# Agent attention and a top-1 mixture of experts: narrower margins of two tests, two left tiles less, banks of products issued in one go

## The chip, the core and the metric

The kernel runs on one core of one Trainium2 chip. The metric is the time of the program on the device in microseconds. Before the change it was 717.3 us, the median of three runs (715.77 to 720.54).

## The reference

Four batches of 11456 tokens with 128 channels. An attention through 49 agents is followed by a mixture of eight experts, of which each token takes one.

```python
a2k = softmax(agents @ k.T * scale)        # 49 x 11456
agent_v = a2k @ v                          # 49 x 128
x = softmax(q @ agents.T * scale) @ agent_v
e_idx = argmax(x @ w_gate)                 # one expert a token
out = probs[e_idx] * sigmoid(x @ w_output_gate)[e_idx] * (relu(x @ w1[e_idx]) @ w2[e_idx])
```

All is f32. The expert's hidden layer has 1024 units.

## The kernel before, in words

A token's x is a mean of the 49 rows of agent_v, so all of a batch's tokens lie close to each other. The kernel uses that twice. First, each batch has one expert that nearly all of its tokens choose (`choose`). Second, most hidden units of that expert have the same sign at every token. `units` ranks the 1024 units by how near to a sign change they can come (`k16`, the squared cosine between a unit's weights and the direction of the mean, in steps). The 256 most doubtful units are computed for each token (the main stream: `mm1`, `relu`, `mm2`). All others are folded into one linear product (`linear`).

Whether a token may use this is tested. `q_rest` computes, for each unit of 1024 tokens (8 tiles of 128), eight gate products `lg` into one bank, and then the products `t` with the next 256 units of the rank, two tiles to a bank. `most` (VectorE) and `beyond` (ScalarE) look whether one of these leaves its sign by the margin SLIGHT (lines 345, 377, 378). For the units behind rank 512 a ball bound holds: `limit` makes `lim` from the unit at rank 512, and `route` compares the token's norm with it (line 1357). A token that fails a test, or that chooses another expert, is a *left* token.

Left tokens are gathered by expert into tiles of 128 and computed in f32 with all 1024 units. `left_table` counts them by phase (a phase is a batch here), `left_index` finds a tile's tokens by indirect DMAs on POOL's queue, `left_load` fetches the expert's weights (SP's queue, 2 x 512 KB), `left_front` makes the transpose `let` and the product `lx` (K = 49), `left_back` the eight products `lh`, two ReLUs, eight products `ly` and a scaling, and `left_store` scatters the rows over the output (POOL's queue). PHASES (line 33) says how many tiles of each phase are in the program: 10, 6, 4 and 1. A group that needs more is computed by a loop at the end (lines 2024 to 2035), which is passed over otherwise.

All instructions are emitted by a planner that is written into the kernel. Each piece of work is a generator that yields what its next instruction reads and writes. `can` (line 117) decides by planned times whether it may be issued; PE's side work has slots that `tick` (line 514) gives between the main stream's products. A generator has a priority: left work has LEFT (line 1872), the scoring products 4. So what is issued where, on every engine, follows from these planned times, and a change of one piece moves the pieces behind it. The engines then run their queues in order.

Of the kernel before, what the change touches and what calls it, by code (L numbers as in the profile page):

```python
# [13 lines left out]
ALU = mybir.AluOpType  # L14
# [4 lines left out]
B, N, C, A, E, F = 4, 11456, 128, 49, 8, 1024  # L19
# [4 lines left out]
ACTIVE = NK * P  # L24
CHOSEN = 2 * ACTIVE
# [4 lines left out]
SCALE = 1.0 / float(C) ** 0.5  # L30

LARGE, SMALL, KEEP = 7, 10, 3
PHASES = [(0, 1, 10, 128), (1, 1, 6, 128), (2, 1, 4, 128), (3, 1, 1, 128)]
ORDER = [0, 1, 3, 2]
NG = B * E
BIG = 1048576.0
# [238 lines left out]
def agent_attention_top1_moe(ctx, tc, qT, kT, v, aT, wg, wo, w1, w2, cst, out):  # L275
    nc = tc.nc
    clk = Clock()
    ACT, DVE, POOL = Engine(clk, "ACT", nc.scalar), Engine(clk, "DVE", nc.vector), Engine(clk, "POOL", nc.gpsimd)
    PE, SY = Engine(clk, "PE", nc.tensor), Engine(clk, "SP", nc.sync)
# [32 lines left out]
    def hold(long=False):  # L312

        k = last[0]
        banks[k][0] = False
        if long:
            long_held.append((k, banks[k][1]))
        return k
# [23 lines left out]

    LONG = 3
    SUMMED = (2, 6)
    SLIGHT = 7.0 / 16.0 * 1.02

    kc = cp.tile([P, K_W], F32, name="kc")
    sel = wk.tile([P, A2], F32, name="sel", tag="sel", bufs=1)
# [6 lines left out]
    def load_constants():  # L355
# [20 lines left out]
        POOL.memset(signed[:, 1:2], 0.5)  # L376
        POOL.memset(slight, SLIGHT)
        POOL.memset(passed, -SLIGHT)
        for u in range(3):
# [41 lines left out]
    for i in range(3):  # L421
        t = cp.tile([P, 8, P], F16, name=f"e16_{i}")
# [5 lines left out]
    for i in range(2):  # L428
        t = cp.tile([P, 2, 18], F16, name=f"gs_{i}")
# [3 lines left out]
    for i in range(2):  # L433
        t = cp.tile([P, E, NCOL], F32, name=f"oht_{i}")
# [8 lines left out]

    efd = [dr.tile([n * N, A2], F32, name=f"efd{b0}") for b0, n, _, _ in PHASES]
    cumd = [dr.tile([n * E * P, NCOL], F32, name=f"cumd{b0}") for b0, n, _, _ in PHASES]
    ppid = [dr.tile([n * E, P], F32, name=f"ppid{b0}") for b0, n, _, _ in PHASES]
    avnd = dr.tile([B, A, C], F32, name="avnd")
    ttd = [dr.tile([r, 8], F32, name=f"ttd{b0}") for b0, _, _, r in PHASES]
    ttid = [dr.tile([r, 8], I32, name=f"ttid{b0}") for b0, _, _, r in PHASES]

# [450 lines left out]
    def units(b, ad, w1t, w2t):  # L901
# [3 lines left out]
        t = bank(f"awp{b}")  # L905
        mark = hold()
        tv = t[:, 0:NB * A].rearrange("p (n a) -> p n a", a=A)
# [12 lines left out]
        u = wk.tile([P, NB], F32, name=f"uu{b}", tag="uu")  # L920
# [18 lines left out]
        yield from DVE.q.reciprocal(iq, q)  # L939
        yield from DVE.q.tensor_tensor(u, u, iq, op=ALU.mult)  # L940
        k16 = wk.tile([P, NB], F16, name=f"k16{b}", tag="k16")
        yield from DVE.q.tensor_scalar(k16, u, 1024.0, 1024.0, op0=ALU.mult, op1=ALU.add)
        calm[0] = b == 0
        key = wk.tile([P, NB], F32, name=f"key{b}", tag="key")
        yield from DVE.q.tensor_tensor(key, k16, unit_no, op=ALU.add)
# [11 lines left out]
        for hf in (1, 0):  # L957
# [4 lines left out]
            t, mark = krs[hf]  # L962
            yield "PE", [k16], [t], 1
            for j in range(HB):
                PE.matmul(t[:, j * P:(j + 1) * P], k16[:, hf * HB + j:hf * HB + j + 1].broadcast_to([P, P]), idf16,
                          start=False, stop=(j == HB - 1))
            chain((below_rows, above_rows)[hf](t, mark, rows[hf], (low, pm)[hf], key, nkey, made), b)
        yield from any_bank()
        t = bank(f"cs{b}")
# [32 lines left out]
        for n in range(NB):  # L1002
            yield from DVE.q.tensor_scalar(pm[:, n], places_, rank[:, n:n + 1], sg[:, n:n + 1], op0=ALU.is_equal,
                                           op1=ALU.mult)
# [6 lines left out]
        for j, (x, c) in enumerate(((st["A16"], CHOSEN), (R16, ACTIVE))):  # L1011
            yield from any_bank()
            t = bank(f"wp{b}_{j}")
# [62 lines left out]
    def limit(b, rank, k16):  # L1076

        while not state[b]["w"]:
            yield None
        x = wk.tile([P, NB], F32, name=f"lmx{b}", tag="lmx")  # L1080
        c = wk.tile([P, 1], F32, name=f"lmc{b}", tag="lmc")
        yield from DVE.q.scalar_tensor_tensor(x, rank, float(CHOSEN), k16, op0=ALU.is_equal, op1=ALU.mult, accum_out=c)
        yield from wait_free()
        r = bank(f"lim{b}")
        mark = hold()
        yield from PE.q.matmul(r[:, 0:1], ones, c, start=True, stop=True)
        lim = wk.tile([P, 1], F32, name=f"lim_{b}", tag="lim")

        yield from DVE.q.tensor_scalar(lim, r[:, 0:1], -A / SLIGHT / 1024.0, A / SLIGHT * (2.0 + 0.5 / 1024.0 + 1e-5),
                                       op0=ALU.mult, op1=ALU.add)  # L1090
        release(mark)
        yield from DVE.q.reciprocal(lim, lim)
        state[b]["lim"] = lim
# [96 lines left out]
    def q_rest(b, u, s, mark):  # L1190
        base, pp, nt = UNITS[u]
        me = len(rests)
        rests.append(0)
        r = group_of(b, u)
        off = 8 * (u - r["units"][0])
        e2, lv, tm = (x[0:pp, off:off + nt] for x in (r["e2"], r["lv"], r["tm"]))
        while not home_ready(b, u) or me > 1 and not state.get(0, {}).get("w"):
            yield None
        sv = s[0:pp, 0:nt * A2].rearrange("p (t a) -> p t a", a=A2)[:, :, 0:A]
        while me > 1 and squared[0] < me - 1:  # L1200
            yield None
        m = wk.tile([P, 8], F32, name=f"qm{b}_{u}", tag="qm", bufs=3)
        yield from DVE.q.tensor_reduce(m[0:pp, 0:nt], sv, axis=AX.X, op=ALU.max)
        z = wk.tile([P, 8, A2], F32, name=f"qz{b}_{u}", tag="qz", bufs=2)
        yield from DVE.q.tensor_tensor(z[0:pp, 0:nt, 0:A], sv,
                          m[0:pp, 0:nt].unsqueeze(2).broadcast_to([pp, nt, A]), op=ALU.subtract)
        release(mark)
        if "ef" not in r:
            r["ef"] = wk.tile([P, 24, A2], F32, name=f"ef{b}_{u}", tag=home(b, u), bufs=1)
        ef = r["ef"][:, off:off + 8, :]  # L1210
        ev = ef[0:pp, 0:nt, 0:A]
        yield from ACT.q.activation(ev, z[0:pp, 0:nt, 0:A], AF.Exp, scale=SCALE)
        e16 = e16s[(NU * b + u) % 3]
        yield from ACT.q.copy(e16[0:pp, 0:nt, 0:A], ev)
        yield from LOW.q.tensor_tensor(e16[0:pp, 0:nt, A:2 * A], ev, e16[0:pp, 0:nt, 0:A], op=ALU.subtract)
        yield from POOL.q.tensor_copy(e16[0:pp, 0:nt, 2 * A:P], ev[:, :, AR:A])
        yield from ACT.q.activation(z[0:pp, 0:nt, 0:A], ev, AF.Square)
        while not r["free"]():
            yield None
        yield from DVE.q.tensor_reduce(e2, z[0:pp, 0:nt, 0:A], axis=AX.X, op=ALU.add)  # L1220
        squared[0] += 1
        while me > 0 and rests[me - 1] < 1:
            yield None
        while vacant_turned() is None:
            yield None
        x1 = place(("x1", b, u), vacant_turned()[1], [1024], F16)
        yield from SY.q.dma_start(x1[:, 0:nt * pp].rearrange("p (t c) -> p t c", c=pp), e16[0:pp, 0:nt, :],
                                  transpose=True)
        X1[b, u] = x1
        rests[me] = 1  # L1230
        while not {"gs", "ndom"} <= state.get(b, {}).keys() or (me > 0 and rests[me - 1] < 2):
            yield None
        gs = state[b]["gs"]
        yield from wait_free()
        lg = bank(f"lg{b}_{u}")
        mark = hold()
        for t in range(nt):
            yield from PE.q.matmul(lg[0:pp, t * 36:(t + 1) * 36], x1[:, t * pp:(t + 1) * pp],
                                   gs.rearrange("p k c -> p (k c)"), start=True, stop=True)
        yield from ACT.q.copy(lv.rearrange("p t a -> p (t a)"), lg[0:pp, 0:nt * 36])  # L1240
        release(mark)
        rests[me] = 2
        while not state[b]["w"] or me > 0 and tested[0] < me:
            yield None
        own_ = state[b]["w"][0][0]
        for h in range(0, nt, 2):
            n = min(2, nt - h)
            yield from wait_free()
            t = bank(f"t{b}_{u}_{h}")
            mark = hold()  # L1250
            tv = t.rearrange("p (t k) -> p t k", k=ACTIVE)
            for k in range(n):
                yield from PE.q.matmul(tv[0:pp, k, :], x1[:, (h + k) * pp:(h + k + 1) * pp], own_[:, ACTIVE:CHOSEN],
                                       start=True, stop=True)
            spawn((most, beyond)[h in SUMMED](tm[:, h:h + n], tv[0:pp, 0:n, :], mark, r), 1)
        tested[0] += 1
        r["efs"][u] = ef, me
        if u == r["units"][-1]:
            spawn(route(b, r), 0)
# [38 lines left out]
    def route(b, r):  # L1298
# [8 lines left out]
        e2, tm, lv = r["e2"][:, 0:nt], r["tm"][:, 0:nt], r["lv"][:, 0:nt]  # L1307
# [8 lines left out]
        while not clk.started:  # L1316
# [12 lines left out]
                                 op0=ALU.is_ge, op1=ALU.mult)  # L1329
# [24 lines left out]
            SM[b, u] = smt[:, 8 * (u - u0):8 * (u - u0) + UNITS[u][2]]  # L1354
        dd = tl("dd")
        yield from DVE.q.scalar_tensor_tensor(dd, d256, state[b]["lim"], d256, op0=ALU.mult, op1=ALU.mult)
        yield from DVE.q.scalar_tensor_tensor(dd, e2, SLIGHT, dd, op0=ALU.mult, op1=ALU.is_ge)
        far = rm
        yield from DVE.q.tensor_tensor(far, tm, passed[:, 0:nt], op=ALU.is_gt)
        yield from DVE.q.tensor_tensor(dd, dd, far, op=ALU.max)  # L1360
# [6 lines left out]
        for u in us:  # L1367
            base, pp, k = UNITS[u]
            ef, me = r["efs"][u]
            yield from POOL.q.tensor_copy(ef[0:pp, 0:k, A], T[0:pp, 8 * (u - u0):8 * (u - u0) + k])  # L1370
            r0 = (b - PHASES[ph][0]) * N + base
            yield from SY.q.dma_start(efd[ph][r0:r0 + pp * k, :].rearrange("(p t) a -> p t a", t=k), ef[0:pp, 0:k, :])
# [496 lines left out]
    left = []  # L1869
    stored = set()  # L1870

    WAYS, LEFT = 2, 5
    left_todo = [(ph, k) for ph, x in enumerate(PHASES) for k in range(x[2])]

    ready = {}
# [217 lines left out]
```

## Time and profile before

| | |
|---|---|
| median of three runs | 717.3 us |
| the profiled execution | 715.21 us |
| its span, first to last instruction | 713.4 us |
| mean granted TensorE clock | 0.969 |
| busy: PE, DVE, ACT, POOL | 655.7, 511.5, 453.9, 265.7 us |

Busy time is the time in which at least one instruction of the engine runs. Records of PE overlap, since products are pipelined: a record's duration is longer than what it adds to the engine's time. What it adds is read from the start of one record to the start of the next. Names: `y`, `h` main stream; `qs`, `ks` scoring products; `av` value products; `lg`, `t` gate products and tests; `wp`, `vp`, `lin` the weights of a batch; `let`, `lx`, `lh`, `ly` left tiles.

### The profile page before, as it was taken

The page shows a single profiled execution, that of the slowest core. Times are in us where ns is not written, and L with a number is a line of the kernel's source. Part 1 is how long each engine was busy: PE and PEld are TensorE (multiplying, and loading weights), DVE is VectorE, ACT ScalarE, POOL GpSimd, SP SyncE. Part 2 cuts the span into 40 slices and gives each one's busy share as a digit, 9 for nine tenths or more (in the row PEclk, how much of TensorE's full clock was granted, in tenths as well). Part 3 has the DMA queues.
Part 4 walks back from the last instruction along what each step waited for, and adds up shares of the span by engine and source line. Part 5 has one row for each costly group of instructions (what it writes and reads, how often), then busy time and mean ns, then how long its engine had stood idle before and what let it go on. Part 6 is the DMA issues. An engine that isn't in the chain of part 4 may idle for free. (4 is left out here: it accounts for less than half of the span.)

```text
span 713.4 us, 23130 instructions
## 1 busy us (share of the span) xinstructions
PE 655.7 (92%) x9031; PEld 545.5 (76%) x9031; DVE 511.5 (72%) x1455; ACT 453.9 (64%) x1314; POOL 265.7 (37%) x482
## 2 busy tenths in 40 slices
PE   9998899979986999989979999899998999999990
PEld 7886688767865676878868888778877779988990
DVE  1665777756897889689877688798788896665330
ACT  2336678736784776875684777787466887566440
POOL 4020026562442268236343543155335353340110
PEclk9999999997998999999999999999999999999996
DMA  8989286699897359995978559665498397627230
GB/s 321 375 228 356 46 203 197 202 299 273 234 259 208 91 165 281 272 298 154 299 165 248 178 189 275 167 176 162 121 294 211 91 240 167 219 83 269 97 123 28
DMA packets 105229, 147.36 MB, mean 207 GB/s; under 512 B 60681, under 2 KB 69729, under 8 KB 105112
## 3 DMA queue, kind: packets, MB, share of 16 engines
q1 hardware_dynamic: 103096, 143.59, 68.6%
q0 software_dynamic: 2016, 2.21, 1.9%
q8 instruction: 73, 1.20, 0.7%
q14 instruction: 44, 0.36, 0.2%
HBM read 99.08 MB, written 35.63 MB: 189 GB/s over the span
## 5 line engine op out<-in xcount | busy, mean ns | idle before, releaser
L225 PE MATMUL y<-vv,hh 128*128 128x128 f16 (+1 forms) x1440 | 178.8, 220 | 0.0
L225 DVE SCALAR_TENSOR_TENSOR hl<-h,hh 128x512 f16<-128x512 f32 (+1 forms) x184 | 122.2, 668 | 65.5 <-ACT hh L225 64.6
L225 PEld LDWEIGHTS <-x_ld 128*128 128x128 f16 (+1 forms) x1440 | 115.7, 100 | 51.1 <-issue 22.0
L225 PE MATMUL y<-vv,hl 128*128 128x128 f16 x720 | 149.0, 221 | 1.3 <-DVE hl L225 1.3
L225 ACT ACTIVATE hh<-h 128x512 f16<-128x512 f32 (+1 forms) x184 | 107.1, 594 | 58.5 <-PE h L225 57.4
L225 PE MATMUL h<-x_ld,w 128*128 128x512 f16 (+1 forms) x368 | 119.9, 378 | 5.4 <-ACT os L225 1.8
L225 PEld LDWEIGHTS <-hh 128*128 128x128 f16 (+1 forms) x1440 | 116.8, 100 | 5.3 <-issue 0.8
L225 PE MATMUL y<-lin,x_ld 128*128 128x128 f16 x720 | 99.9, 221 | 6.8 <-DVE tm L225 2.5
L225 ACT ACTIVATE t<-t,slight 128x256 f32<-128x256 f32 x176 | 79.5, 455 | 10.3 <-PE t L225 9.8
L225 POOL TENSOR_TENSOR e<-ef,e 128x392 f16<-128x392 f32 (+1 forms) x48 | 42.2, 880 | 93.1 <-ACT e L225 79.1
L225 PEld LDWEIGHTS <-hl 128*128 128x128 f16 x720 | 72.8, 101 | 4.5 <-DVE hl L225 1.6
L225 PE MATMUL t<-w,x_ld 128*128 128x256 f16 x360 | 70.2, 279 | 4.3 <-DVE hl L225 3.0
L225 PE MATMUL lh<-lxs,lw_ld 128*128 128x128 f32 x336 | 71.3, 298 | 0.5 <-DVE tm L225 0.5
L225 PE MATMUL ly<-lw_ld,lh 128*128 128x128 f32 x336 | 71.0, 298 | 0.0
L225 PEld LDWEIGHTS qs<-at,q_ld 128*64 128x64 f32 x1440 | 50.6, 142 | 23.7 <-DMA q_ld<-qT 12.0
L225 PE MATMUL qs<-at,q_ld 128*64 128x50 f32 x1440 | 58.2, 229 | 11.2 <-DMA q_ld<-qT 10.0
L225 ACT ACTIVATE os<-y,smt 128x128 f32<-128x128 f32 (+1 forms) x182 | 52.3, 369 | 20.9 <-PE y L225 16.8
L225 DVE TENSOR_REDUCE tm<-t 128x2 f32<-128x512 f32 (+1 forms) x92 | 61.7, 679 | 4.6 <-PE t L225 4.3
L225 PEld LDWEIGHTS ks<-at,k_ld 128*64 128x64 f32 x1440 | 48.7, 139 | 11.3 <-issue 4.7
L225 PE MATMUL ks<-at,k_ld 128*64 128x50 f32 x1440 | 56.0, 226 | 1.4 <-DMA k_ld<-kT 1.2
L225 PEld LDWEIGHTS lh<-lxs,lw_ld 128*128 128x128 f32 x336 | 53.1, 192 | 2.6 <-DVE tm L225 0.6
L225 PEld LDWEIGHTS ly<-lw_ld,lh 128*128 128x128 f32 x336 | 52.7, 192 | 1.3 <-issue 0.5
(320 smaller groups left out, 1329.6 us busy)
## 6 DMA issues: line engine op xcount, KB each, us to landing
v_ld<-v SPq DMA_DIRECT2D x44, 516.0 KB
q_ld<-qT SPq DMA_DIRECT2D x44, 512.0 KB
out<-os SPq DMA_DIRECT2D x88, 256.0 KB
k_ld<-kT SPq DMA_DIRECT2D x43, 512.0 KB
lw_ld<-w SPq DMA_DIRECT2D x42, 512.0 KB
efd<-ef SPq DMA_DIRECT2D x44, 200.0 KB
w2t<-w SPq DMA_DIRECT2D x4, 512.0 KB
w1t<-w SPq DMA_DIRECT2D x3, 512.0 KB
```

The lines of the kernel that those rows point to most:

```text
L225: return getattr(self.eng, op)(*a, **k)
```

## The change

The margin SLIGHT goes from 0.446 to 0.129. The rank's steps become four times finer: the squared cosine is rounded to multiples of 1/4096 instead of 1/1024, by adding and taking away 1.5 x 2^23, which takes one DVE operation more. The ball bound follows these steps, and SLIGHT is no longer a factor on both of its sides. PHASES has 9, 6, 3 and 1 tiles: one less for the first and one for the third phase. The gate products of a bank, and the two products of a test's bank, are asked for once and then issued without a break. LEFT is 4.

```diff
-PHASES = [(0, 1, 10, 128), (1, 1, 6, 128), (2, 1, 4, 128), (3, 1, 1, 128)]
+PHASES = [(0, 1, 9, 128), (1, 1, 6, 128), (2, 1, 3, 128), (3, 1, 1, 128)]
...
-    SLIGHT = 7.0 / 16.0 * 1.02
+    SLIGHT = (23.0 * 7.0 / 2048.0 + 49.0 / 1024.0) * 1.02
+    WHOLE = 1.5 * 2.0 ** 23
...
-        yield from DVE.q.tensor_scalar(k16, u, 1024.0, 1024.0, op0=ALU.mult, op1=ALU.add)
+        yield from DVE.q.tensor_scalar(u, u, 4096.0, WHOLE - 2048.0, op0=ALU.mult, op1=ALU.add)
+        yield from DVE.q.tensor_scalar(k16, u, WHOLE, None, op0=ALU.subtract)
...
-        yield from DVE.q.tensor_scalar(lim, r[:, 0:1], -A / SLIGHT / 1024.0, A / SLIGHT * (2.0 + 0.5 / 1024.0 + 1e-5),
+        yield from DVE.q.tensor_scalar(lim, r[:, 0:1], -A / 4096.0, A * (0.5 + 0.5 / 4096.0 + 1e-5),
...
+        yield "PE", [x1, gs], [lg], 1
         for t in range(nt):
-            yield from PE.q.matmul(lg[0:pp, t * 36:(t + 1) * 36], x1[:, t * pp:(t + 1) * pp],
-                                   gs.rearrange("p k c -> p (k c)"), start=True, stop=True)
+            PE.matmul(lg[0:pp, t * 36:(t + 1) * 36], x1[:, t * pp:(t + 1) * pp],
+                      gs.rearrange("p k c -> p (k c)"), start=True, stop=True)
...
+            yield "PE", [x1, own_], [t], 1
             for k in range(n):
-                yield from PE.q.matmul(tv[0:pp, k, :], x1[:, (h + k) * pp:(h + k + 1) * pp], own_[:, ACTIVE:CHOSEN],
-                                       start=True, stop=True)
+                PE.matmul(tv[0:pp, k, :], x1[:, (h + k) * pp:(h + k + 1) * pp], own_[:, ACTIVE:CHOSEN],
+                          start=True, stop=True)
...
-        yield from DVE.q.scalar_tensor_tensor(dd, e2, SLIGHT, dd, op0=ALU.mult, op1=ALU.is_ge)
+        yield from DVE.q.tensor_tensor(dd, e2, dd, op=ALU.is_ge)
...
-    WAYS, LEFT = 2, 5
+    WAYS, LEFT = 2, 4
```

The first place is PE's queue in the last batch, at the gate products of a late unit. Before:

```order
L225 MATMUL let_3_11431<-kc,big_0_8522 49x128
L225 LDWEIGHTS x_10_ld
L225 MATMUL lg_10_11400<-gs_113,x_10_ld 128x36
...
L225 LDWEIGHTS hl_11241
L225 MATMUL y_11380<-vv_9728,hl_11241 128x128
L225 LDWEIGHTS x_10_ld
L225 MATMUL lg_10_11400<-gs_113,x_10_ld 128x36
L225 LDWEIGHTS x_1_ld
L225 MATMUL y_11380<-lin_103,x_1_ld 128x128
```

And now, of a bank of the same batch, with the eight gate products in a row (six of them left out):

```order
L225 MATMUL lh_3_0_11248<-lxs_3_11209,lw_30_0_ld 128x128
L225 LDWEIGHTS x_8_ld
L225 MATMUL lg_8_11124<-gs_113,x_8_ld 128x36
...
L225 LDWEIGHTS x_8_ld
L225 MATMUL lg_8_11124<-gs_113,x_8_ld 128x36
L225 LDWEIGHTS hl_11155
L225 MATMUL y_11234<-vv_9552,hl_11155 128x128
```

Single gate products among the `y` have become one block between two of them.

The second place is PE's queue at the start of the second batch, where its weights `wp` are made. Before:

```order
L225 MATMUL qs_4_4184<-at,q_4_ld 64x50 x16
L225 MATMUL ppt_4296<-kc,ppi_4287 8x128
L225 LDWEIGHTS A_4003
L225 MATMUL wp_0_4338<-pm_3884,A_4003 128x512
...
L225 MATMUL qs_5_4323<-at,q_5_ld 64x50 x16
L225 LDWEIGHTS A_4003
L225 MATMUL wp_0_4338<-pm_3884,A_4003 128x512
...
L225 MATMUL lin_4360<-w2t_3336,awm_4352 98x128
L225 LDWEIGHTS R_92
L225 MATMUL wp_1_4399<-pm_3884,R_92 128x256
```

And now:

```order
L225 MATMUL km_11_r<-km_11_d,ones 128x50
L225 MATMUL qs_5_4287<-at,q_5_ld 64x50 x16
L225 LDWEIGHTS A_3988
L225 MATMUL wp_0_4396<-pm_3938,A_3988 128x512
...
L225 MATMUL av_0_4436<-v_0_ld,ev_0_4389 64x129 x8
L225 LDWEIGHTS R_92
L225 MATMUL wp_1_4472<-pm_3938,R_92 128x256
...
L225 MATMUL av_1_4453<-v_1_ld,ev_1_4424 64x129 x8
```

The scoring product `qs_5` stood behind six of the eight first `wp`; it now stands ahead of all eight, and two value products `av` stand among the `wp` that follow.

The third place is the end of PE's queue, at the last left tile. Before, one of its last products `ly` and what stands around it:

```order
L225 LDWEIGHTS x_10_ld
L225 MATMUL y_12973<-lin_103,x_10_ld 128x128
L225 MATMUL ly_0_12952<-lw_00_0_ld,lh_0_1_12947 128x128
L225 LDWEIGHTS hh_12903
L225 MATMUL y_12973<-vv_9728,hh_12903 128x128
```

And now, the last `y` and the rest of the queue ahead of the loop:

```order
L225 LDWEIGHTS hl_12857
L225 MATMUL y_12904<-vv_9552,hl_12857 96x128
L225 MATMUL lx_0_12926<-let_sb_0_12908,lav_0_12780 128x128
L225 MATMUL lh_0_0_12937<-lxs_0_12935,lw_00_0_ld 128x128 x4
L225 MATMUL lh_0_1_12944<-lxs_0_12935,lw_00_0_ld 128x128 x4
L225 MATMUL ly_0_12951<-lw_00_0_ld,lh_0_0_12942 128x128 x4
L225 MATMUL ly_0_12951<-lw_00_0_ld,lh_0_1_12949 128x128 x4
```

The last left tile's products, which stood among the `y`, now stand together behind the last one.

## Rows read from the trace of the kernel before

**Rows 1.** The page: busy us, share of the span, instructions; the granted clock.

```profile
PE 655.7 (92%) x9031; PEld 545.5 (76%) x9031; DVE 511.5 (72%) x1455; ACT 453.9 (64%) x1314; POOL 265.7 (37%) x482
...
PEclk9999999997998999999999999999999999999996
```

**Rows 2.** Windows: length; PE, PEld, DVE, ACT, POOL busy (instructions); clock, DMA, GB/s.

```profile
340.00:580.00 240.00, 225.89 (x2867) 188.94 (x2864) 195.98 (x584) 168.65 (x512) 104.45 (x168) 0.98 0.71 199
580.00:629.60 49.60, 49.44 (x505) 44.16 (x502) 34.95 (x102) 33.88 (x101) 21.02 (x39) 1.00 0.73 189
629.60:697.10 67.50, 67.46 (x740) 59.78 (x740) 29.51 (x85) 36.41 (x97) 10.38 (x13) 1.00 0.44 146
```

**Rows 3.** Timeline of PE, left tiles: start us, duration us, engine, operation, records.

```profile
662.22 0.44 PE L225 MATMUL lh<-lxs,lw_ld 128*128 128x128 f32 x2
662.50 0.22 PE L225 MATMUL y<-vv,hl 128*128 128x128 f16 x1
...
684.46 0.27 PE L225 MATMUL let<-kc,big 128*49 128x128 f32 x1
684.57 0.22 PE L225 MATMUL y<-vv,hl 128*128 128x128 f16 x1
...
685.82 0.48 PE L225 MATMUL lx<-let_sb,lav 49*128 49x128 f32 x2
686.24 0.23 PE L225 MATMUL y<-vv,hl 128*128 128x128 f16 x1
```

**Rows 4.** Groups: count | busy us, mean ns of one | idle before, what ended it.

```profile
L225 PE MATMUL lh<-lxs,lw_ld 128*128 128x128 f32 x336 | 71.3, 298 | 0.5 <-DVE tm L225 0.5
L225 ACT ACTIVATE lh<-lh 128x512 f32<-128x512 f32 x42 | 25.4, 604 | 16.1 <-PE lh L225 15.7
L225 POOL DMA_INDIRECT out<-big,ltg_0s x9 | 9.1, 1010 | 53.3 <-ACT big L225 22.7 <-DMA lw_ld<-w 14.2 <-SPq L2025 13.9
```

**Rows 5.** Timelines of ACT, POOL, PE and DVE at the end; in brackets idle before.

```profile
685.22 0.37 ACT L225 ACTIVATE big<-ly,big 128x128 f32<-128x128 f32 x1 [0.19 <-PE ly L225]
...
685.86 0.98 POOL L225 DMA_INDIRECT out<-big,ltg_0s  x1 [4.49 <-ACT big L225]
...
694.89 0.37 ACT L225 ACTIVATE big<-ly,big 128x128 f32<-128x128 f32 x1 [1.38 <-PE ly L225]
...
696.87 0.22 PE L225 MATMUL y<-vv,hl 128*96 128x128 f16 x1
...
697.12 0.42 DVE L225 TENSOR_TENSOR os<-y,smt 96x256 f32<-96x256 f32 x1 [1.07 <-PE y L225]
...
700.72 0.98 POOL L225 DMA_INDIRECT out<-big,ltg_0s  x1 [13.88 <-SPq L2025]
```

**Rows 6.** Timelines of PE, POOL and SP: the last batch's table, gather, loads.

```profile
629.63 0.39 PE L225 MATMUL pexc<-tot,kc 128*128 128x8 f32 x2 [0.19 <-DVE tot L225]
...
664.60 1.05 POOL L225 DMA_INDIRECT big<-efd,ltu_0s  x1 [0.88 <-POOL big L225]
...
677.79 0.32 SPq L225 DMA_DIRECT2D lav<-avnd  x1
```

**Rows 7.** Timeline of DVE, choice of units in the first batch.

```profile
63.78 0.17 DVE L225 TENSOR_SCALAR sg<-sg 128x8 f32<-128x8 f32 x1
```

**Rows 8.** Timeline of PE, gate products of the third batch.

```profile
371.58 0.22 PE L225 MATMUL lg<-gs,x_ld 128*128 128x36 f16 x2 [2.64 <-DMA x_ld<-e]
...
371.86 0.26 PE L225 MATMUL lg<-gs,x_ld 128*128 128x36 f16 x4
371.96 0.27 PE L225 MATMUL y<-lin,x_ld 128*128 128x128 f16 x2
```

**Rows 9.** Timeline of PE at the second batch's start, and windows as in rows 2.

```profile
229.60 1.95 PE L225 MATMUL qs<-at,q_ld 128*64 128x50 f32 x32 [5.93 <-DMA q_ld<-qT]
...
225.87:232.70 6.83, 3.10 (x36) 2.57 (x37) 3.87 (x11) 1.20 (x3) 2.48 (x4) 0.50 0.66 191
...
540.00:560.00 20.00, 16.87 (x205) 13.84 (x204) 16.40 (x42) 13.66 (x44) 10.85 (x14) 0.91 0.54 152
```

## The prediction

> **What bounds the kernel now.** Read the page's busy times first: PE is busy 655.7 us of a span of 713.4, DVE 511.5, ACT 453.9 [rows 1]. The line of PEclk beside it shows where the granted clock fell, now and then. An average hides stages, so the windows come next [rows 2]. From 580 us to the last matmul at 697.1 PE is busy 49.44 + 67.46 = 116.9 of 117.1 us: nothing but TensorE work sets the end there, and a microsecond of it is a microsecond of time. From 340 to 580 us it is busy 225.9 of 240, 94%. Left tiles run only in these stretches; ahead of 340 there are none.
>
> The end has a tail that PE doesn't set [rows 5]. The last matmul ends at 696.87 + 0.22 = 697.1, DVE scales its bank until 697.5, the store follows, and POOL's last scatter starts at 700.72 although its tile was ready at 694.89 + 0.37 = 695.3. POOL idled 13.88 us ahead of it. The releaser that the row names is SP's branch, which sends no data; both write the output tensor, and I read the wait as one for the last stores. From that scatter to the end of the span it is 12.7 us, whatever comes before.
>
> **Does the table fit?** The static tiles are only enough if the tokens that are left fit into them. Counted from the reference's inputs in double precision, with the tests as the code writes them, before has 834 / 522 / 295 / 77 left tokens. In the first batch one expert's group holds 129, in the third one holds 258: one and two tokens over a multiple of 128. With the new margins these become 124 and 251, so the tiles needed are 9 / 6 / 3 / 1, which is the new table. The runtime loop stays unused unless rounding moves 5 tokens one way.
>
> **Two left tiles less.** A tile has 16 f32 products of 128x128, one of K = 49 and one transpose. In the dense stretch a product shows as two records and moves the next instruction 0.28 us on (662.22 to 662.50) [rows 3]; 16 of them are 4.5 us. The K = 49 product takes 0.42 (685.82 to 686.24), the transpose 0.11 (684.46 to 684.57): 5.0 us for a tile. The row's mean of 298 ns is not used, since records overlap [rows 4].
> - The third phase's tile ran after 629 us, where PE was never idle: the full **-5.0 us**.
> - The first phase's tile ran between 340 and 580. With PE busy 94% I expect 0.94 x 5.0 = 4.7, less a little, since a filler also covers waits: **-4.3 us**; the ends are 0 (it only filled waits) and -5.0.
>
> The Trainium skill (Perfetto Trace Analysis, Identifying the Most-Contended Engine) calls matmul busy time a bad measure and asks for the busy share of LDWEIGHTS. By that measure the middle stretch is 188.9 of 240, 79%, the last one 59.8 of 67.5, 89% [rows 2]; the first tile would then pay about 3.9 and the other 4.5, and the sum below would be 1 us smaller. The trace can't yet say which is nearer.
>
> What goes with the tiles on other engines is hidden. On ACT that is 4 activations of 604 ns and 6 short copies or scalings, on SP 4 loads of 512 KB, on POOL 6 indirect DMAs of about 1.05 us [rows 4]. None of these engines is over 64% busy but DVE, which gains nothing here but index arithmetic. If the cover went, 6 POOL steps would be 6 us of POOL.
>
> **The last tile moves behind the main stream.** Before, its products were woven into the y products and ended at 694.8. Now, as the order of PE shows, only its transpose stands among the last y; its other 17 products follow the last y. So the total of PE's work is unchanged by that, but the tail changes. The lone tile hands over once without cover: K = 49 product, copy of 0.27 us on ACT, first product, about 0.4 us that PE waits. The four products ahead cover the second ReLU (0.60 us against 4 x 0.28 = 1.1). In exchange its scatter comes right after its own scaling: 0.09 + 0.37 + 0.27 = 0.7 us after PE's end (685.22 + 0.37 to 685.86 is the 0.27) [rows 5], instead of 3.6 now. The main stores have then landed, as they have some 5.3 us from the last y. Sum: +0.4 - 2.9 = **-2.5 us**. The ends are -2.9, and +3 if the tile isn't ready: from the table of the last batch (629.63) to its transpose (684.46) it took 54.8 us, with a gather at 664.60 that waited in POOL's queue behind a scatter [rows 6]. From that table to the last y it was 67.5 us. Less the tile that is gone and the one that now stands behind, 2 x 5.0, some 57 us are left, hardly more than it took.
>
> **The rest.** One DVE operation more in each choice of units: 0.17 us for 128x8 [rows 7], 4 times; only the first batch's, where no main stream runs yet, lies on the path: **+0.2**. The far test's scalar_tensor_tensor becomes a tensor_tensor, 16 times one small DVE operation for another: 0. The gate products and tests that are issued in one go are as many as before. Four gate products took 0.10 us until the next matmul (371.86 to 371.96) [rows 8], so eight in a row are 0.2 us in which a y must wait, and four tests are 0.44. This is work moved, not added: 0, with bounds of +3 (48 banks by 0.06) and -3, as the planner's light slots are freed for other work. The starts of the left tiles' loads move up in the planner's order (5 to 4, their fronts to 3); each queue holds the same kinds of loads, and I price it at 0.
>
> **Sum:** -5.0 - 4.3 - 2.5 + 0.2 = -11.6. The profiled execution took 715.2 us, so 703.6; the median of the runs shown, 717.3, is 2.1 above that, and I forecast **705.5 us**.
>
> **The rivals.** The planner writes a new order from the first unit on, so the waits of the middle are drawn anew. What one costs is seen at the second batch's start [rows 9]: PE is in order, and a scoring product waited 5.93 us for its q load with the rest of the weight products queued behind it. The clock stood at half, 1.2 GHz, from 225.87 to 232.70; of that the 3.1 us after 229.6 were at work, worth another 1.5. One such event is **7.4 us**.
> - *That wait goes too.* The new order scores the keys of the batch ahead earlier, puts eight weight products in one piece behind the scoring product, and has more work between the choice of the expert and the first main product. It can hide what is now waited for: 705.5 - 7.4 = 698. Against it: a scoring product on the same load still stands ahead of the weight products. Chance 0.18.
> - *The fillers are missed.* In the middle the left tile covered waits: it pays 0 instead of 4.3, the tail pays 0, and one more stall brings half clock. The window from 540 us has a mean clock of 0.91 [rows 9], which is 3.6 us of 20 at half, worth 1.8. Sum: 703.6 + 4.3 + 2.5 + 1.8 = 712.2 in the profile, 714 by the median. For it: PE waited 2.64 us for a transposed load ahead of 371.58 [rows 8], although left work was at hand. The Trainium skill (TensorE: Matmul & The Clock Gate, The HAM clock gate) has half clock as the default that activity lifts; by it less filler in front of a wait is a loss in itself. The trace agrees so far that after the wait of 5.93 us the clock was at half. Chance 0.24.
> - *Slower: loads ahead of the weight products.* In the new order two value products stand among the weight products of the second batch, each on its own load and exponentials; before there were none. Each start of a batch could then wait as long as the one that is seen. From three more events of 7.4 us on, the gain of 11.6 turns into a loss of 10.6: 728. One or two leave it at or below the old time. Against it: these values were loaded long before, as the loads stand early in SP's order. Chance 0.07.
> - *The table doesn't fit.* If the first or third batch needs the tile after all, the loop runs it alone: at most the 35.0 us from table to gather, 8.0 from the loads (677.79) to the K = 49 product (685.82), 9.4 from there to the end of its scaling (695.26) [rows 3, 5, 6]. That is some 52 us, so about 757. Chance 0.01.
>
> **How the numbers follow.** The forecast holds 0.50, between 701 and 710, its own bounds. What a measurement of this kernel can tell from no change is about 1%, 7.2 us: faster is below 710.1, slower above 724.5. The forecast and the first rival lie below, the second is within. Faster 0.68, same 0.24, slower 0.08. The range must leave no more than 2 in 10 out: from 696, below the first rival, to 716, above the second.
>
> **What will show it.** 304 records of lh and of ly instead of 336; PE's busy time lower by some 10 us or more; from 580 us to the last matmul no idle time, and the end of PE near 687; the last scatter under 1 us after PE's end and with its own scaling as releaser; the branch at the end passing over the loop. The prediction is wrong if PE's idle time ahead of the last matmul, 41.4 us now (713.4 - 655.7, less the 16.3 of the tail), grows by more than 5, or if the last tile waits for its gather or its weights.

## The result, and the profile after

The changed kernel takes **690.9 us** (median of 4 runs, 690.65 to 691.18) against 717.6 for the one before in the same comparison: a ratio of 0.963, 95% interval 0.959 to 0.966. The forecast of 705.5 had the sign right and the size wrong; 690.9 lies below its range. The profiled execution has a span of 689.2, 24.2 less than before.

The signs named in advance came, but two of them far too strongly: PE's busy time fell by more than it was to, and PE ended at 674.8 instead of near 687. First the page of the changed kernel (busy us, share, instructions; granted clock), to be held against [rows 1]:

```profile
PE 639.1 (93%) x8962; PEld 531.1 (77%) x8962; DVE 501.5 (73%) x1455; ACT 454.7 (66%) x1327; POOL 257.0 (37%) x473
...
PEclk9999999999998999999999999999999999999996
```

PE is busy 16.6 us less, where two tiles are 10.0. The clock line has one dip left in the middle where [rows 1] has two. The groups of the left tiles show 304 records of each product instead of 336, as forecast [rows 4]:

```profile
L225 PE MATMUL ly<-lw_ld,lh 128*128 128x128 f32 x304 | 64.4, 303 | 0.0
L225 PE MATMUL lh<-lxs,lw_ld 128*128 128x128 f32 x304 | 62.7, 296 | 0.4 <-ACT lxs L225 0.4
```

The last batch's table is the best landmark, since nearly the same work stands ahead of it in both kernels: 312 products h in both, 2404 and 2407 records y, 488 and 480 of lh and ly. PE's timeline of the changed kernel has it here:

```profile
615.42 0.34 PE L225 MATMUL pexc<-tot,kc 128*128 128x8 f32 x2
```

And its windows, columns as in [rows 2], the second and third parted at that table:

```profile
340.00:580.00 240.00, 227.18 (x2845) 192.37 (x2842) 188.68 (x584) 171.86 (x520) 102.83 (x171) 0.99 0.73 198
580.00:615.40 35.40, 34.93 (x375) 30.80 (x375) 24.58 (x79) 23.92 (x75) 16.81 (x29) 1.00 0.42 141
615.40:674.80 59.40, 58.68 (x682) 50.96 (x679) 29.77 (x88) 34.07 (x90) 5.32 (x6) 1.00 0.46 156
```

That table came at 629.63 before [rows 6] and comes at 615.42 now: **14.2 us ahead, with only 8 left records less** done by then (4 products of 0.28 us, with one transpose and one K = 49 product some 1.6 us). Behind it PE has 59.4 us to go instead of 67.5, so the two tiles appear there, 8.1 us. The rest of the gain was there already, and beyond these 1.6 us it isn't left work. From the table on PE is full but for 0.7 us.

The end, timelines of PE, ACT and POOL (in brackets idle before and its releaser), to be held against [rows 5]:

```profile
668.64 0.27 PE L225 MATMUL let<-kc,big 128*49 128x128 f32 x1
...
670.06 0.48 PE L225 MATMUL lx<-let_sb,lav 49*128 49x128 f32 x2 [0.36 <-ACT let_sb L225]
...
670.90 2.05 PE L225 MATMUL lh<-lxs,lw_ld 128*128 128x128 f32 x16 [0.35 <-ACT lxs L225]
...
672.79 2.01 PE L225 MATMUL ly<-lw_ld,lh 128*128 128x128 f32 x16
...
674.88 0.37 ACT L225 ACTIVATE big<-ly,big 128x128 f32<-128x128 f32 x1 [1.30 <-PEq L2029]
675.52 0.98 POOL L225 DMA_INDIRECT out<-big,ltg_0s  x1 [18.53 <-ACT big L225]
```

The lone last tile is as forecast: two hand-overs without cover, 0.71 us (I had 0.4), and the scatter 0.7 us behind PE's end, released by its own scaling. The tail is 14.4 us after 16.3, since from the scatter to the end it is now 13.7 us (12.7 before).

**Where the 24.2 us came from.** PE's time up to its last matmul is busy plus idle time, and I count work at half clock as taking twice as long. (That is near: from the start of a tile's 16 products lh to the start of the product behind them it took 3.47 us in e18, at a granted clock of 0.51 (693.66 to 697.13), and 1.89 in the change, at 1.00 (670.90 to 672.79), so 1.8 times as long.) So a span is: PE's busy time at full clock, plus half of its busy time in stretches with a granted clock of 0.50, plus its idle time, plus the tail. Before: 643.1 + 12.7 + 41.4 + 16.3 = 713.4 (rounded). After: 632.8 + 6.3 + 35.7 + 14.4 = 689.2. That is **-10.3 work, -6.3 half clock, -5.7 idle, -2.0 tail**. My sum had the first and the last, 9.3 and 2.5, and none of the two in the middle.

For the table that follows: a row's terms are of one execution, and those of e10 and e16 were slower than their medians (724.2 and 728.7 us), so their terms are somewhat high.

### The profile page after: what moved, and what is told of

It is laid out like the page before. It is cut to its first block, busy times and chain, and to the rows that moved or that the text cites. A ratio compares the mean times of both kernels' runs of the same rounds, so it can differ in the third digit from the quotient of the medians.

```text
span 689.2 us, 22947 instructions
## 1 busy us (share of the span) xinstructions
PE 639.1 (93%) x8962; PEld 531.1 (77%) x8962; DVE 501.5 (73%) x1455; ACT 454.7 (66%) x1327; POOL 257.0 (37%) x473
## 5 line engine op out<-in xcount | busy, mean ns | idle before, releaser
L225 PE MATMUL y<-vv,hh 128*128 128x128 f16 (+1 forms) x1440 | 173.8, 219 | 0.0
L225 PEld LDWEIGHTS <-x_ld 128*128 128x128 f16 x1440 | 104.6, 98 | 54.7 <-issue 27.8
L225 PE MATMUL y<-vv,hl 128*128 128x128 f16 x720 | 146.2, 219 | 0.0
L225 PE MATMUL h<-x_ld,w 128*128 128x512 f16 (+1 forms) x368 | 116.1, 375 | 2.7 <-DVE hl L225 1.5
L225 ACT ACTIVATE os<-y,smt 128x128 f32<-128x128 f32 (+1 forms) x208 | 60.5, 372 | 23.1 <-PE y L225 21.1
L225 PE MATMUL t<-w,x_ld 128*128 128x256 f16 x360 | 60.3, 273 | 6.0 <-DVE os L225 1.4
L225 PE MATMUL ly<-lw_ld,lh 128*128 128x128 f32 x304 | 64.4, 303 | 0.0
L225 PEld LDWEIGHTS qs<-at,q_ld 128*64 128x64 f32 x1440 | 50.7, 141 | 16.1 <-issue 4.6
L225 PE MATMUL lh<-lxs,lw_ld 128*128 128x128 f32 x304 | 62.7, 296 | 0.4 <-ACT lxs L225 0.4
L225 PEld LDWEIGHTS ly<-lw_ld,lh 128*128 128x128 f32 x304 | 48.0, 196 | 2.1 <-issue 0.8
L225 PE MATMUL av<-v_ld,ev 128*64 128x129 f32 x720 | 49.2, 279 | 0.4 <-DVE lim L225 0.2
```

The costliest lines, as they stand in the source:

```text
L225: return getattr(self.eng, op)(*a, **k)
```

## The experiments

Two explanations stood against each other: that something in the change closes waits (banks in one go, fewer tiles, LEFT), or that the planner draws all waits anew with any edit, and this draw was lucky. So parts were done alone, and the order was redrawn with the work unchanged, by one number of the planner's model. The table has all 20 kernels, with the span's four terms from each profile (us). *Values* is when the second batch's value products av begin, counted from the first main product; *idle 1-2* is PE's idle time from the first main product to the first one of the second batch, #92, without the wait directly ahead of that one. The ratios below are against before in the same comparison, where its median was 715.4 to 717.6.

| kernel | median | values | idle 1-2 | work | half clock | idle | tail |
|---|---|---|---|---|---|---|---|
| **21 tiles** | | | | | | | |
| before | 717.6 | 46.1 | 16.5 | 643.1 | 12.7 | 41.4 | 16.3 |
| e1_margins | 720.8 | 46.1 | 15.5 | 644.2 | 15.5 | 39.2 | 17.4 |
| e5_before_186 | 720.2 | 46.1 | 14.0 | 644.9 | 11.2 | 41.5 | 19.3 |
| e6_before_194 | 728.8 | 46.1 | 16.7 | 642.1 | 22.1 | 43.3 | 18.2 |
| e3_banks | 719.4 | 34.3 | 11.0 | 648.1 | 9.0 | 37.3 | 21.1 |
| e12_old_table | 714.3 | 34.3 | 11.6 | 643.3 | 10.6 | 42.9 | 15.8 |
| **19 tiles, not both in one go** | | | | | | | |
| e2_tiles | 703.8 | 46.1 | 15.9 | 634.3 | 7.8 | 42.1 | 17.2 |
| e9_tiles_186 | 718.8 | 46.1 | 17.4 | 635.4 | 17.9 | 49.1 | 16.1 |
| e10_tiles_194 | 716.9 | 46.1 | 14.0 | 634.0 | 26.5 | 45.6 | 16.3 |
| e11_no_banks | 699.6 | 46.1 | 15.0 | 634.7 | 11.5 | 36.6 | 14.9 |
| e14_gates_only | 707.3 | 47.5 | 14.4 | 632.6 | 14.6 | 40.1 | 14.6 |
| e13_tests_only | 710.4 | 35.3 | 12.1 | 634.7 | 14.8 | 48.9 | 14.3 |
| e16_four_slots | 720.2 | 35.6 | 13.8 | 637.0 | 25.7 | 51.4 | 12.8 |
| **19 tiles, both in one go** | | | | | | | |
| after | 690.9 | 34.3 | 11.7 | 632.8 | 6.3 | 35.7 | 14.4 |
| e4_left5 | 691.6 | 34.3 | 10.6 | 633.5 | 6.8 | 32.0 | 17.5 |
| e7_after_186 | 702.6 | 34.6 | 9.8 | 637.3 | 10.3 | 37.8 | 14.3 |
| e8_after_194 | 691.3 | 34.3 | 10.9 | 631.2 | 10.6 | 33.0 | 14.8 |
| e15_slots_paid | 691.7 | 35.4 | 9.5 | 635.7 | 3.4 | 31.1 | 19.8 |
| e18_paid_lone_tail | 712.3 | 33.3 | 8.5 | 636.6 | 12.4 | 50.2 | 12.7 |
| e17_values_held | 725.1 | 47.6 | 14.7 | 635.4 | 19.5 | 50.7 | 17.6 |

**The parts alone.** e1 is the kernel before with the margins of the change (its lines on SLIGHT, WHOLE, k16, lim and dd) and the old table:

```diff
-    SLIGHT = 7.0 / 16.0 * 1.02
+    SLIGHT = (23.0 * 7.0 / 2048.0 + 49.0 / 1024.0) * 1.02
...
```

e2 is e1 with the new table:

```diff
-PHASES = [(0, 1, 10, 128), (1, 1, 6, 128), (2, 1, 4, 128), (3, 1, 1, 128)]
+PHASES = [(0, 1, 9, 128), (1, 1, 6, 128), (2, 1, 3, 128), (3, 1, 1, 128)]
```

e3 is the kernel before with both kinds of banks in one go, lg as here and t alike:

```diff
+        yield "PE", [x1, gs], [lg], 1
         for t in range(nt):
-            yield from PE.q.matmul(lg[0:pp, t * 36:(t + 1) * 36], x1[:, t * pp:(t + 1) * pp],
+            PE.matmul(lg[0:pp, t * 36:(t + 1) * 36], x1[:, t * pp:(t + 1) * pp],
...
```

e4 is the change with the old LEFT:

```diff
-    WAYS, LEFT = 2, 4
+    WAYS, LEFT = 2, 5
```

> The kernel before with the narrow margins alone: the table of left tiles stays at 10, 6, 4, 1, banks product by product, LEFT 5. Theory 'work' (two tiles less are worth more than their products): no tile goes, so 717.5 to 718. Theory 'banks' (products of a bank in one go close the waits of the middle): nothing of it is here, 717.5 to 718. Theory 'redraw' (any edit draws the planner's order anew, and the waits with it): anywhere from 705 to 725, with waits for q loads and half clock at other places than before.

> Narrow margins and the table 9, 6, 3, 1; banks product by product and LEFT 5 as before. Work: the whole gain of 26.7 us, so about 691. Banks: only the two tiles and the tail, my 11.6, so about 706, with the wait of some 6 us for the q load at the second batch's start still there. Redraw: 706 with a spread of some 10 to either side, and other waits than in before and in the change.

> The kernel before with only the gate products and the tests of a bank in one go; wide margins, 21 tiles, LEFT 5. Work: 717.5. Banks: some 14 us less, about 703, PE's waits for q loads down from 10 us to some 2 and half clock from 31 us to some 14. Redraw: 717.5 with a spread of some 10 to either side.

> The changed kernel with LEFT 5 in place of 4: everything else of the change. Work and banks: 691, within 2. A theory that LEFT gives what I did not price: 703 to 705. Redraw: 691 with a spread of some 10, upwards rather than downwards, as the change's draw was a lucky one.

Measured: e1 1.003 of before (0.9998 to 1.006), e2 0.979 (0.974 to 0.984), e3 1.003 (1.000 to 1.007), e4 0.962 (0.957 to 0.968). The tiles alone gave what I had forecast for the tiles, the banks alone nothing, and together they gave 26: neither theory of a single part fits. LEFT back at 5 gives the same time, in this one order, as priced.

**Redraws.** One number, in before (e5, e6), in the change (e7, e8) and in e2 (e9, e10), 186 or 194:

```diff
-    AFTER = {"PE": 190.0, "ACT": 120.0, "DVE": 150.0, "POOL": 120.0, "SP": 0.0}
+    AFTER = {"PE": 186.0, "ACT": 120.0, "DVE": 150.0, "POOL": 120.0, "SP": 0.0}
```

> The kernel before with one number of the planner's model changed, the delay it assumes behind a TensorE result, 186 ns in place of 190: same work, another order. Theory 'together' (banks in one go pay off once the two tiles are gone, by a mechanism, whatever the draw): within 4 us of 717. Theory 'redraw' (each new order has its own waits): 10 us or more away from 717 in one of the redraws of before, tiles or change, and the groups overlap.

> As the run before it, with 194 ns. Together: within 4 us of 717. Redraw: somewhere from 705 to 728.

> The changed kernel with 186 ns in place of 190 in the planner's model: same work, another order. Together: 691 within 4, PE's idle time ahead of the last matmul 32 to 36 us. Redraw: 691 was a lucky draw, so the others come out higher, 695 to 708, with idle times of 36 to 44.

> As the run before it, with 194 ns. Together: 691 within 4. Redraw: 695 to 708.

> Narrow margins and the table 9, 6, 3, 1, banks product by product, LEFT 5, with 186 ns in the planner's model. Known by now: five orders of 21 tiles took 717 to 729, four of 19 tiles with banks in one go 691 to 703, one of 19 without 704. Theory 'tiles' (two tiles are worth some 25 us on the average, more than my 11.6, and banks nothing): this lies among the orders with banks, 691 to 704. Theory 'together' (banks in one go are worth some 12 once the tiles are gone): 704 to 712, above those with banks.

> As the run before it, with 194 ns. Tiles: 691 to 704. Together: 704 to 712.

Measured against before: 1.007 (1.004 to 1.011), 1.019 (1.014 to 1.024), 0.978 (0.969 to 0.987), 0.967 (0.963 to 0.971), 1.001 (0.998 to 1.005), 0.999 (0.996 to 1.002). In each of the three the same work in another order moves the time, by up to 11 to 15 us. Of the change's two, e7 came out where 'redraw' had it, and e8 where 'together' had it. e2's agreement with my sum was luck too: its two redraws show no gain at all.

**Banks out, table back.** e11 takes e3's diff (lg and t) back out of the change, e12 e2's:

```diff
 e11
-        yield "PE", [x1, gs], [lg], 1
...
 e12
-PHASES = [(0, 1, 9, 128), (1, 1, 6, 128), (2, 1, 3, 128), (3, 1, 1, 128)]
+PHASES = [(0, 1, 10, 128), (1, 1, 6, 128), (2, 1, 4, 128), (3, 1, 1, 128)]
```

> The changed kernel with banks product by product again, LEFT 4. Tiles: 691 to 704. Together: 704 to 712.

> The changed kernel with the old table 10, 6, 4, 1 (two of the 21 tiles run on padding alone). Tiles: 717 to 729, as the other orders of 21 tiles. Together: as banks give nothing without the tiles gone, 715 to 721. A theory that margins and banks carry it, by the tests' smaller cost: 700 or less.

Measured: 0.977 (0.973 to 0.981) and 0.995 (0.991 to 0.998). The column *work* settles the tiles: 642 to 648 with 21, 631 to 637 with 19, means 644.3 (6 kernels) and 634.7 (14), **9.6 us for the two tiles**, whatever the order. Neither theory held: e11 at 699.6 lies in the range of 'tiles' and below that of 'together', e9 and e10 at 718.8 and 716.9 lie above both, and e12 at 714.3 below both.

**What the banks do.** In all eight orders with both kinds product by product the second batch's values begin 46.1 us after the first main product. PE's timeline of before there, with the key maximum (km_t, km_r) and the first value product:

```profile
108.84 0.27 PE L225 MATMUL km_t<-kc,m 128*50 128x128 f32 x1
...
114.33 0.42 PE L225 MATMUL km_r<-km_d,ones 50*128 50x50 f32 x2
...
122.20 1.10 PE L225 MATMUL av<-v_ld,ev 128*64 128x129 f32 x16
```

The same rows of the change:

```profile
100.42 0.27 PE L225 MATMUL km_t<-kc,m 128*50 128x128 f32 x1
...
102.56 0.42 PE L225 MATMUL km_r<-km_d,ones 50*128 50x50 f32 x2
...
110.67 1.10 PE L225 MATMUL av<-v_ld,ev 128*64 128x129 f32 x16
```

The values come 11.5 us earlier. In before PE later stands still ahead of a scoring product; its timeline:

```profile
152.86 0.22 PE L225 MATMUL lg<-gs,x_ld 128*128 128x36 f16 x2
156.76 0.44 PE L225 MATMUL qs<-at,q_ld 128*64 128x50 f32 x8 [3.69 <-DMA q_ld<-qT]
```

Two windows of before (columns as in [rows 2]) show the clock at 0.50 behind it:

```profile
152.00:158.00 6.00, 2.31 (x67) 2.06 (x64) 1.17 (x2) 1.28 (x4) 3.35 (x7) 0.97 1.03 392
158.00:164.00 6.00, 5.08 (x35) 3.40 (x34) 3.46 (x8) 2.89 (x7) 0.00 (x0) 0.50 1.18 271
```

The same windows of the change, full and at full clock:

```profile
152.00:158.00 6.00, 5.92 (x96) 4.56 (x94) 4.47 (x8) 5.07 (x19) 2.89 (x5) 1.00 1.01 339
158.00:164.00 6.00, 5.96 (x88) 4.45 (x86) 5.52 (x18) 3.98 (x13) 2.50 (x4) 1.00 1.07 245
```

This wait, 3.5 to 4.7 us, is in all eight orders with both kinds product by product, and in none of the six first orders with both in one go. Which of the two edits, and how:

```diff
 e13: the change, with
-        yield "PE", [x1, gs], [lg], 1
...
 e14: the change, with
-            yield "PE", [x1, own_], [t], 1
...
 e15: the change, with
+        paid = min(light, owed[0])
+        owed[0] -= paid
-        clk.slots = [0, light, 0]
+        clk.slots = [0, light - paid, 0]
...
+        owed[0] += nt - 1
...
 e16: e11, with
-    def tick(heavy=1, light=2):
+    def tick(heavy=1, light=4):
```

> The changed kernel with only the tests t in one go, the gate products lg one by one. Known by now, in 14 orders: with banks product by product (8) the second batch's value products begin 46.1 us after the first main product, PE then waits 3.6 to 5.1 us for a q load some 77 us after it, and idle time plus half-clock loss is 48 to 72 us; with banks in one go (6) 34.3 to 34.6, no such wait, 39 to 54. In this kernel's order the values stand at the 26th to 28th main product, as in the change; if that is what counts: 34 to 36, no q wait, sum 39 to 54, 690 to 704. If the gate products carry it: 46, a q wait of 4, 700 to 719.

> The changed kernel with only the gate products lg in one go, the tests two by two as before. Its order has the second batch's values at the 40th main product, as the orders without banks. If the tests carry it: 46 us, a q wait of 3.6 to 5, sum 48 to 72, 700 to 719. If the gate products do: no q wait, 690 to 704.

> The changed kernel, whose banks are issued in one go but pay for it: the planner's light slots that the 7 or 1 further products would have taken are withheld from the side work of the next turns. Theory 'slots' (the change frees two light slots a turn for other side work): the values come late again, 46 us, a q wait of 4, 700 to 719. Theory 'hold' (a PSUM bank that is filled at once is given back sooner, and the key maximum's products, which wait for a free bank, come sooner): 34 to 36, no q wait, sum 39 to 54, 690 to 704.

> The changed kernel with banks product by product, but four light slots in a turn of the side work instead of two: a bank is filled in half as many turns. Hold, and slots too: the values early, 34 to 38 us after the first main product, no q wait, sum 39 to 54, 690 to 704, without any bank in one go. If only issuing a whole bank in one piece helps: 46, a q wait of 4, 700 to 719.

Measured: 0.994 (0.990 to 0.997), 0.986 (0.982 to 0.990), 0.968 (0.961 to 0.975), 1.006 (1.002 to 1.009). The tests bring the values forward (35.3), the gates don't (47.5, with a q wait of 0.6 only). Paid slots leave them early, so it isn't the slots that are freed; four slots bring them early without any bank in one go. That fits a PSUM bank which is filled faster and given back sooner, but no view shows who holds a bank, so this stays argued. And **early values don't make a fast kernel**: e13 and e16 have them and took 710 and 720. e16's time went to new waits, such as this one in its timeline:

```profile
302.74 1.01 PE L225 MATMUL h<-x_ld,w 128*128 128x512 f16 x2 [5.30 <-DVE avs L225]
```

**The early values held back, and an attempt to win more.** e17 is the change with a pause ahead of the second batch's key maximum; e18 is e15 with 188 in the planner's model:

```diff
+        if b == 1:
+            yield from pause(10000.0)
         m1 = wk.tile([P, A2], F32, name=f"m1_{b}_{n}", tag="m1")
```

> The changed kernel with both kinds of banks in one go, but the second batch's key maximum held back by 10 us of the planner's time, so that its values begin at the 40th main product, as in all eight orders with both kinds product by product. If the early values are what takes the q wait and the half clock out of the first two batches: values at some 46 us after the first main product, a q wait of 3 to 5 us around 150, idle time over the first two batches 14 to 17 instead of 10 to 12. For the whole: 695 to 706 if that loss lasts; 691 if it is made up for later. If the early values are only a sign of something else: no q wait, idle 10 to 12.

> Banks in one go with paid slots (as e15_slots_paid) and 188 ns in the planner's model, which in its order puts a lone last tile behind the main stream, as in the change. In e15_slots_paid PE was done at 670.2, 4.6 us earlier than in the change, but the tail was 19.8 instead of 14.4, as two scatters stood behind each other there. If the new draw keeps the middle: PE's end near 670 to 675 and a tail of 14 to 15, 685 to 691. By the spread of redraws: anywhere from 686 to 703.

Measured: 1.011 (1.005 to 1.017) and 0.992 (0.989 to 0.996). In e17 the loss of the first two batches came back as expected, idle 14.7 and 6.8 us of half clock from 159 on, but through another wait, ahead of a value product and not of a scoring product. Its timeline of PE:

```profile
155.10 0.60 PE L225 MATMUL t<-w,x_ld 128*128 128x256 f16 x4
158.19 0.44 PE L225 MATMUL av<-v_ld,ev 96*64 96x129 f32 x4 [2.49 <-DVE hl L225]
```

(The row names DVE's hl, which this product doesn't read; what it waited for stays open.) So the price comes with late values here too, and the q load is only one place where it is paid; e14 agrees, with late values, idle 14.4 and a q wait of 0.6 only. How late values lead to these waits I didn't follow from link to link. The other 20 us and more of e17's loss lie outside the first two batches, nearly all of it behind them: the whole order had been redrawn again. e18 missed as well: among other waits its lone last tile was not ready, waiting for the load of its batch's agent rows (lav) and then 3.10 us (SP's branch, named as releaser, sends no data; I take it for the weights). Its timeline of PE at the end:

```profile
690.10 0.46 PE L225 MATMUL lx<-let_sb,lav 49*128 49x128 f32 x2 [0.99 <-DMA lav<-avnd]
693.66 3.63 PE L225 MATMUL lh<-lxs,lw_ld 128*128 128x128 f32 x16 [3.10 <-SPq L2035]
697.13 2.01 PE L225 MATMUL ly<-lw_ld,lh 128*128 128x128 f32 x16
```

No kernel beat the change; e4, e8 and e15 equal it.

## Why the prediction was wrong

- **Two left tiles: right in size.** Priced at 9.3, measured 9.6 over 20 orders and 10.3 in the pair. Where I placed the first tile's part was off: nearly all of both showed behind the last table. What a tile covered by filling waits can't be told: these numbers are PE's work alone, and the idle time is 40.9 us on the average with 21 tiles and 41.7 with 19, in a spread of 31 to 51. By the busy share of LDWEIGHTS, which the Trainium skill (Perfetto Trace Analysis, Identifying the Most-Contended Engine) asks for in place of matmul busy time when TensorE's headroom is judged, my estimate was 8.4. For the same reason the traces don't decide between the two.
- **The tail: right in kind.** The scatter came 0.7 us behind PE's end, as described. But "it is 12.7 us, whatever comes before" was wrong: from the last scatter to the end it is 13.7 here, 12.9 in e15 and 14.1 in e8. So the tail gave -2.0, and with 0.71 us of hand-overs in place of 0.4 the term is -1.3 for -2.5 (the 0.71 stand in the idle time). It isn't a property of the change: in e4 and e15 the tail is 17.5 and 19.8. The bound of +3 for a last tile that isn't ready was real, as e18 shows.
- **Margins, the DVE operation, LEFT:** nothing that can be told from a redraw (e1 at 720.8, e4 at 691.6).
- **The sum's last step.** 703.6 + 2.1 is 705.7, not 705.5; and the 2.1 by which before's median lay above its profiled execution was not there in the change (690.9 and 691.0).
- **"This is work moved, not added: 0, with bounds of +3 (48 banks by 0.06) and -3": the step that failed.** The work was only moved; PE's work at full clock fell by the tiles alone. But I priced the moved products by their own time, and not by what moves with them. In the pair what I had at 0 came to -12.0: half clock -6.3, idle -5.7. And redraws with the work unchanged move the time by up to 15 us (e2 at 703.8, e9 at 718.8), so this is a term of its own that the products' time can't give. The part of it in the first two batches is the best supported: kernels with late values have 14.0 to 17.4 us of idle time there, those with early ones 8.5 to 13.8, on the average 15.4 against 11.0. With it goes the time at half clock between 120 and 200 us, 3.4 to 10.2 us against 0 to 3.4. In the pair this is -4.8 idle and -4.7 half clock (9.32 us of work at half clock from 157.60 on, now none). It doesn't show in when the second batch starts: #92 comes 162.9 us after the first main product in before and 164.6 in the change, but PE was busy for 145.7 us in between then and is for 152.9 now. What was saved went into work done ahead.
- **Rival 1 was the right kind, with the wrong event.** The wait at the second batch's start shrank from 5.93 us to 2.08, with a new one of 1.78 just ahead of it, and half clock stayed there, with more work in it (5.82 us for 3.10). PE's timeline of the change:

```profile
218.49 0.39 PE L225 MATMUL km_r<-km_d,ones 50*128 50x50 f32 x2 [1.78 <-DVE km_d L225]
...
220.96 1.95 PE L225 MATMUL qs<-at,q_ld 128*64 128x50 f32 x32 [2.08 <-DMA q_ld<-qT]
```

and the stretch at half clock around it:

```profile
219.95:226.78 6.83, 5.82 (x44) 3.23 (x46) 5.95 (x20) 1.38 (x3) 2.09 (x3) 0.50 0.44 98
```

What went was the earlier wait, at 153 us, with the 10.24 us of half clock behind it; neither stood in my sum or among my rivals.

- **The range was too narrow for any point forecast of this kernel.** Orders of the same 19 tiles took 691 to 725, of the same 21 tiles 714 to 729. I had seen that "the waits of the middle are drawn anew" and still gave the draw one event of 7.4 us.

**What stays open.** Whether banks in one go are better beyond the first two batches. With 19 tiles and both in one go, e17 left aside, the six medians have a mean of 696.7, the other seven 711.0, but they overlap (712.3 against 699.6), and several of the fast orders are near copies of the change's (e8's clock falls to half within 0.7 us of the change's at 219.95, 455.47 and 523.74). With 21 tiles the means are 716.9 (2 kernels) and 721.9 (4). So of the 26.7 us some 10 are shown to be the two tiles, in whatever order. Of the others, 2 are this order's tail, some 9 are the first two batches, where the values come early, and the rest can't be told from a lucky order.

## What to carry to other kernels

In a kernel whose order a planner writes, an edit has two effects: its own work, which rows of the trace price well (here 9.3, measured 9.6), and a new draw of all waits, which no row prices. Measure the second by redrawing the order with the work unchanged, two or three times before and after, and compare work, half clock, idle time and tail apart, from more than one execution each. An operand that the next batch needs (here the key maximum) is worth looking for: what holds it up can show as an idle PE somewhere else, as e17 bears out, and here some 40 us later.

## What the hardware showed that I had not expected

Half clock cost 3.4 to 26.5 us in these kernels, and 6.3 of the 24.2 us gained. In before the wait of 3.69 us at 153 was followed by 10.24 us at 0.50, at 1.2 instead of 2.4 GHz, in which PE was busy 9.32: the loss behind the wait, 4.7 us, is more than the wait. The Trainium skill (TensorE: Matmul & The Clock Gate, The HAM clock gate) has half clock as the default that activity lifts. Most traces agree so far that stretches at half clock follow waits, but not all: in e5 (columns as in [rows 2]) one came while PE had not been idle.

```profile
460.50:467.38 6.88, 6.88 (x81) 5.07 (x81) 6.72 (x31) 6.87 (x26) 2.51 (x4) 1.00 0.19 57
467.38:470.79 3.41, 3.41 (x26) 2.74 (x23) 3.34 (x13) 2.94 (x10) 1.04 (x1) 0.50 1.00 247
```

Nor does the order of PE's products alone set it. Up to the first main product PE's products stand in the same order in the change, e4, e7, e12, e14 and e17, and yet half clock cost 0 us there in the change, 1.7 in e4, e7 and e12, and 3.4 in e14 and e17. The change and e17, from 50 to 76 us:

```profile
50.00:76.00 26.00, 22.63 (x394) 18.26 (x389) 15.92 (x61) 15.88 (x42) 2.22 (x5) 1.00 0.84 287
...
50.00:76.00 26.00, 23.70 (x388) 18.56 (x388) 15.04 (x57) 15.11 (x41) 2.22 (x5) 0.87 0.85 295
```

So differences of some 3 us in the column *half clock* are not to be read as an effect of an edit; the 10.3 of work and the 4.7 at 157.60 are larger.

In e15 the last two scatters into the output tensor ran behind each other. PE was done 4.6 us earlier there than in the change, yet the tail is 5.4 us longer. The first of the two began 3.4 us after PE's end, and the last pieces of the chain that ended last (start us, length us) show its landing, 2.71 us, ahead of the second (whether the program alone asks for that order no run shows):

```profile
673.60 2.71 DMA out<-big,ltg_0s
676.31 0.02 issue
676.34 0.02 POOLq L225
676.36 0.52 issue
676.87 0.50 POOLq L2034
677.37 0.69 POOL out L225
```
